# Wide tiles of a fused attention and ReGLU kernel: P1 seeded in PSUM under P2, and two quarters multiplied on VectorE straight from PSUM

## The chip, the cores and the metric

The kernel runs on one core of one Trainium2 chip. The metric is the device time of one execution in microseconds, 316.74 before the change (median of three runs, 316.7 to 316.8). Engines are named as in the profile: PE (TensorE, matmul), ACT (ScalarE), DVE (VectorE), POOL (GpSimd), SP (SyncE, which issues DMAs).

## What is computed

Sliding-window attention over 8 batches of 576 positions, 8 heads of 64, then a gated feed-forward layer on the 4608 tokens:

```python
scores = scale * np.matmul(q, k.transpose(0, 1, 3, 2))
mask = (rel >= 0) & (rel < 64)
attn = softmax(np.where(mask, scores, -1e9))
x = concat_heads(np.matmul(attn, v))          # [4608, 512]
gate = np.maximum(x @ w_gate, 0.0)            # w_gate, w_val: [512, 1536]
val = x @ w_val
out = gate * val @ w_out                      # w_out: [1536, 512]
```

## The kernel before

**Tiles.** The tokens are cut into ten tiles: tiles 0 to 3 have 384 tokens and are called narrow here, tiles 4 to 9 have 512 and are the wide ones. For a narrow tile `hidden` forms gate and value directly. For a wide tile `fast_hidden` (L555) uses a Winograd form of Strassen's scheme: seven products instead of eight, called P1 to P7, each on a half of the 512 features, a half of the tokens (256) and a half of the hidden units. Sums of weights (`us`, `vs`, made by `w_form`) and of activations (`xc`, made by `x_form`) are prepared ahead. Then `fast_output` (L667) multiplies by `w_out`, 128 tokens at a time, 12 matmuls of 512 columns each. Between these four output blocks lie the attention steps of later tiles: `values` (two per wide tile) and `scores` (two per wide tile).

**Products and quarters.** The hidden units go in three pieces, j = 0, 1, 2. For each j every product is run for the gate (i = 0) and for the value (i = 1); each time it is four matmuls of 256 columns into one PSUM bank. These four matmuls are called a group here, so a wide tile has 3 x 7 x 2 = 42 groups. P1, P6, P7 and P4 add up in one bank, "A" (L572), P2 is alone in "B", P5 and P3 add up in "C". The four quarters of a piece (half of the units, n, by half of the tokens, h) come from them so:

- n=0, h=0 is P1 + P2. ACT copies A after P1 into an SBUF tile `pr` (`snap`, L593 to L601); DVE adds bank B to it (`add`, L603, the sum at L609); ACT applies relu to the gate's sum (L615); POOL multiplies gate by value into `g_sb` (L620).
- n=0, h=1: A after P6 is copied likewise, and C after P3 is added; relu and multiplication as above.
- n=1, h=1: A after P7, plus C after P5; likewise.
- n=1, h=0 is A after P4: ACT reads both banks into SBUF, the gate with relu (`direct`, L630), and POOL multiplies (L637).

So a piece has on ACT six copies, three relus of sums and two L630; on DVE six sums; on POOL four multiplications.

P6 may overwrite A only when the copy of P1 is done, P7 when the copy of P6 is, P4 when the copy of P7 is; P3 may go on top of P5 only when DVE has read C for the P7 sum (L573).

**What sets the order.** A small planner, `Weaver`, runs while the program is written. It keeps a clock and a heap of events with due times; `W.at(t, fn)` adds one, and before each group `W.advance` issues all events that have come due, in the order of their times. Each group advances the clock by 4 x 263 / 2400 = 0.4383 us, each output matmul by 519 / 2400 = 0.216 us, `values` by 0.62 and `scores` by 0.72. So a wide tile is 42 x 0.4383 + 2 x 0.62 + 2 x 0.72 + 48 x 0.216 = 31.47 us long to the planner. The order in which instructions are issued to one engine is the order in which they run on it: ACT, DVE and POOL are queues.

The q and k transposes on DVE (L195, four for a batch) are such events too. `ahead(t)` (L874) puts them at the start of wide tile t plus `WIDE_T` = 32.69 us plus the slots 0.2, 3.4, 7.6 and 13.8, so for tiles 4 and 5 they fall into the hidden parts of tiles 5 and 6. Those that fall into tile 4 are planned at the start of tile 3, plus 27.6 and the same slots. To the planner tile 3 is 24 x 4 x 391 / 2400 + 36 x 0.216 = 23.43 us long (scores and values that are issued out of the heap do not advance the clock). Tiles 7 to 9 have no q and k transposes.

**Order of the products.** For j = 0: P1, P2, P6, P5, P7, then P1 of j = 1, P4, P3. For j = 1 and 2: P6, P2, P7, P5, P4, then P1 of the next j (if any), P3.

**PSUM banks.** There are eight banks of 128 x 512 fp32. `bank()` (L371) hands out the free bank that was freed longest ago; `free.append` gives one back at the moment when its last reader is issued. A matmul with `start=True` opens a new sum in a bank, and those without it add. `fast_hidden` opens A with P1, B with P2 and C with P5.

The names in the profile: `pr` is the SBUF tile of a pair (gate, value), `bank` a PSUM bank, `g_sb` the gated product in f16, `pw` the exponentials of the scores, `o_sb` an output block on its way to HBM. L588 is the matmul of all products, L679 the output matmul of wide tiles, L396 the exponential of the wide tiles' scores.

Of the kernel before, what the change touches and what calls it, by code (L numbers as in the profile page):

```python
# [47 lines left out]
def kernel(  # L48
# [10 lines left out]
    nc = tc.nc  # L59
# [187 lines left out]
    def st_tiles(u):  # L247
        d = units.setdefault(u, {})
        if u == 0:
            d["st"] = [one_bank() for _ in range(G)]  # L250
        else:
            halves = [two_banks() for _ in range(2)]
            d["st"] = halves[0] + halves[1]
        d["p"] = [None] * G

    def st_block(to, g, hh, n, biased=False):
# [46 lines left out]
    def u_pv(u, hhs=(0, 1), banks=None):  # L303

        d = units[u]
        if "pv" not in d:
            if banks:
                d["pv"] = [one_bank() for _ in range(2)]
            else:
                d["pv"] = two_banks()  # L310
        for hh in hhs:
            to = d["pv"][hh]
            for w in range(UB):
                b, vw = divmod(UB * u + w, NG)
                for s in range(2):
                    for j in range(G):
                        c = VW * (2 * w + s)
                        nc.tensor.matmul(  # L318
                            to[32 * j:32 * j + 32, c:c + D + 1], p_of(u, G * hh + j, w)[:, 32 * s:32 * s + 32],
                            v16s[b % 2][:, vw, G * hh + j, 0:D + 1],  # L320
                            start=True, stop=True, skip_group_check=True)
        return 0.27 * len(hhs)
# [44 lines left out]
    quads = {}  # L367
    wides = {}
    free = []

    def bank():  # L371

        while not free:
            W.pop()
        return free.pop(0)

    def read(to, give):
        unread.discard(id(to))
# [6 lines left out]
    def q_st(qd, banks=None):  # L385

        d = quads[qd] = {"st": banks or [bank() for _ in range(G)], "p": [None] * G}
        unread.update(map(id, d["st"]))
        run_rows([[st_block(d["st"][g][:, 256 * hh + 64 * i:256 * hh + 64 * i + 64], g, hh, q_window(qd, i))
                   for hh in range(2) for i in range(QW)] for g in range(G)])  # L390
        return 0.72
# [19 lines left out]
    def t_pv(t, hh, banks, give):  # L411

        if t not in wides:
            wides[t] = {"pv": {}, "give": give, "x": a_n.tile([128, 2, WS, 2, D // 2], FP16, name="xw", bufs=1),
                        "r": a_n.tile([128, 2, WS, 1], FP32, name="rw")}
        d = wides[t]
        d["pv"][hh] = banks
        unread.update(map(id, banks))
        for qh in range(2):
            qd = 2 * (t - NS) + qh  # L420
            while quads[qd].get("masked", 0) < G:
                W.pop()
            for i in range(QW):
                b, vw = divmod(q_window(qd, i), NG)
                for s in range(2):
                    n = 2 * (QW * qh + i) + s
                    to = banks[n // BS][:, VW * (n % BS):]
                    for j in range(G):
                        nc.tensor.matmul(to[32 * j:32 * j + 32, 0:D + 1],  # L429
                                         quads[qd]["p"][j][:, QW * hh + i, 32 * s:32 * s + 32],  # L430
                                         v16s[b % 2][:, vw, G * hh + j, 0:D + 1],
                                         start=True, stop=True, skip_group_check=True)
# [82 lines left out]
    def hidden(t, spans, f0=0, f1=NF, each=1):  # L515

        if t not in gs:
            gs[t] = g_sb_p.tile([128, NF, WT], FP16, name="g_sb"), {}
        g_sb, done = gs[t]
        xt = xt_tile(t)  # L520
        n = spans[0][1] - spans[0][0]

        w = 512 // n
        each = max(each, w)

        def part(tile):
            return tile[:, 0:w * n].rearrange("p (w n) -> p w n", w=w)

        def relu(r_sb, h1):
            nc.scalar.activation(part(r_sb), part(h1), ACT.Relu)  # L530

        def gate(f, c0, r_sb, h2):
            nc.vector.tensor_tensor(g_sb[:, f:f + w, c0:c0 + n], part(r_sb), part(h2), MUL)  # L533
            done.update(dict.fromkeys(range(f, f + w), c0 + n))

        for fb in range(f0, f1, each):
            r2s = [f_sb.tile([128, 2, WT], FP32, name="pr", bufs=6) for _ in range(2)]
            r_sbs = {}
            for i, wt in enumerate((wg, wv)):
                for c0, f in ((c0, f) for c0, _ in spans for f in range(fb, fb + each, w)):  # L540
                    h = one_bank()
                    for b in range(w):
                        W.advance(W.clock)
                        w_need(wt, f + b)
                        for c in range(NC):
                            nc.tensor.matmul(h[:, b * n:b * n + n], wt[:, c, (f + b) * 128:(f + b) * 128 + 128],  # L546
                                             xt[:, c, c0:c0 + n], start=(c == 0), stop=(c == NC - 1))
                        W.clock += 4 * (n + 7) / 2400.0
                    if i == 0:
                        r_sb = r_sbs[c0, f] = r2s[len(r_sbs) // 2][:, len(r_sbs) % 2]  # L550
                        W.at(W.clock, lambda r_sb=r_sb, h=h: relu(r_sb, h))
                    else:
                        W.at(W.clock, lambda f=f, c0=c0, r_sb=r_sbs[c0, f], h=h: gate(f, c0, r_sb, h))

    def fast_hidden(t):  # L555
# [14 lines left out]
                    "P6": (sums[:, 1, :, c], xc[:, 1]), "P7": (sums[:, 2, :, c], xc[:, 2])}[name]  # L570

        TO = {"P1": "A", "P6": "A", "P7": "A", "P4": "A", "P2": "B", "P5": "C", "P3": "C"}  # L572
        AFTER = {"P6": ("P1", "snap"), "P7": ("P6", "snap"), "P4": ("P7", "snap"), "P3": ("P7", "sum")}  # L573

        def product(j, name, i):
            W.advance(W.clock)
            if name in AFTER:
                before, what = AFTER[name]
                while (j, what, before, i) not in at:
                    W.pop()  # L580
            first = name in ("P1", "P2", "P5")
            if first:
                at[j, TO[name], i] = bank()
            to = at[j, TO[name], i]
            w, x = operands(name, *kinds[i], j)
            for m in range(2):
# [2 lines left out]
                                     start=(first and m == 0 and k == 0), stop=(k == 1), skip_group_check=True)  # L589
            W.clock += 4 * (HT + 7) / 2400.0  # L590
            at[j, "ran", name, i] = True

        def snap(j, name, i):  # L593
            if i == 0:
# [5 lines left out]
                at[j, "snap", name, i] = True  # L600
            W.at(W.clock, copy)  # L601

        def add(j, name, bank_name, i, n, h, delay):  # L603

            def summed():
                while (j, "snap", name, i) not in at:
                    W.pop()
                pr, to = at[j, "pair", name], at[j, bank_name, i]
                nc.vector.tensor_tensor(pr[:, i], to, pr[:, i], ADD)  # L609
                at[j, "sum", name, i] = True  # L610
                if name != "P7":
# [3 lines left out]
                        nc.scalar.activation(pr[:, 0], pr[:, 0], ACT.Relu)  # L615
                    W.at(W.clock + 1.1, relu)
                else:
                    def mult():
                        f = 2 * j + HF * n
                        nc.gpsimd.tensor_tensor(gh[:, f:f + 2, h], pair(pr[:, 0]), pair(pr[:, 1]), MUL)  # L620
                        done[f, h] = done[f + 1, h] = True
                    W.at(W.clock + 1.2, mult)
            W.at(W.clock + delay, summed)

        def direct(j, i):
            if i == 0:
                at[j, "r"] = f_sb.tile([128, 2, WT], FP32, name="pr", bufs=6)

            def copy():
                nc.scalar.activation(at[j, "r"][:, i], at[j, "A", i], ACT.Copy if i else ACT.Relu)  # L630
                free.append(at[j, "A", i])
                if i == 1:
                    W.at(W.clock + 0.7, mult)

            def mult():
                f = 2 * j + HF
                nc.gpsimd.tensor_tensor(gh[:, f:f + 2, 0], pair(at[j, "r"][:, 0]), pair(at[j, "r"][:, 1]), MUL)  # L637
                done[f, 0] = done[f + 1, 0] = True
            W.at(W.clock, copy)

        def step(j, name):
            for i in range(2):
                product(j, name, i)
                if name in ("P1", "P6", "P7"):
                    snap(j, name, i)
                if name == "P2":
                    add(j, "P1", "B", i, 0, 0, 0.1)
                if name in ("P5", "P7") and (j, "ran", "P5", i) in at and (j, "ran", "P7", i) in at:
                    add(j, "P7", "C", i, 1, 1, 0.1 if name == "P5" else 0.8)
                if name == "P4":  # L650
                    direct(j, i)
                if name == "P3":
                    add(j, "P6", "C", i, 0, 1, 0.1)

        last = NF // 4 - 1
        step(0, "P1")
        for j in range(last + 1):
            for name in ("P2", "P6", "P5", "P7") if j == 0 else ("P6", "P2", "P7", "P5"):
                step(j, name)
            tail = [(j, "P4"), (j + 1, "P1"), (j, "P3")] if j else [(j + 1, "P1"), (j, "P4"), (j, "P3")]  # L660
            for jj, name in tail:
# [5 lines left out]
    def fast_output(t, between):  # L667

        g_sb, done = gs[t]
        for sub, before in enumerate(between):  # L670
            for fn in before:
                fn()
            op = bank()
            for i, f in enumerate(F_LAST):
                if i % 4 == 0:
                    W.advance(W.clock)
# [26 lines left out]
        W.at(W.clock, evac)  # L703

    def op_tile():
        return one_bank()

    def output(t, subs=None):
        for sub in range(widths[t] // 128) if subs is None else subs:
# [262 lines left out]
```

## Time and profile before

| | |
|---|---|
| time, median of 3 runs | 316.74 us |
| span of the profiled execution, first to last instruction | 315.2 us |
| granted TensorE clock, mean over the span | 1.000 |
| ACT busy in the stretch 220.72 to 239.32 us (hidden part of tile 7) | 16.86 of 18.60 us |
| DVE busy in the same stretch | 10.70 us |
| POOL busy in the same stretch | 12.03 us |
| DVE busy in the stretch 156.04 to 175.04 us (hidden part of tile 5) | 14.92 of 19.00 us |

The span is 1.5 us shorter than the median of the timed runs, which include what lies around the instructions. A line of the groups reads: line, engine, operation, output and inputs with their shapes, count | busy time in all, mean ns of one | idle time of the engine just ahead of them and what ended it. A line of the timeline reads: start in us, length in us, engine, line, operation, output and input, and how many instructions are merged into it. A busy PE is read off the starts of its groups, since matmuls are pipelined and the length shown for a group overlaps that of the next.

### The profile page before, as it was taken

The numbers are of one execution on the slowest core, as the hardware profiler recorded it, in microseconds if no ns is written. First come the engines' busy times: TensorE is split into PE (matmuls) and PEld (weight loads), VectorE is DVE, ScalarE is ACT, GpSimd is POOL, SyncE is SP. The second block draws the span as 40 slices with busy tenths as digits, with TensorE's granted clock in tenths as the row PEclk, the third lists the DMA queues.
The fourth block names the chain that finished last, engine by engine and source line by source line (L and its number), as shares of the span: only waits on it lengthen the run. The fifth ranks groups of instructions, "written<-read, shape, count | busy, mean of one in ns | idle before, by whom it ended". The sixth has DMA issues, their size and how long they took to land.

```text
span 315.2 us, 10195 instructions
## 1 busy us (share of the span) xinstructions
PE 303.3 (96%) x4295; PEld 210.6 (67%) x4295; DVE 225.9 (72%) x413; ACT 190.1 (60%) x382; POOL 204.9 (65%) x214
## 2 busy tenths in 40 slices
PE   4899989999999998999999999999999999999995
PEld 2575947756556555885588558854886488648854
DVE  6937983786895987989788877898468846845630
ACT  3645324533616616993889378946895689529951
POOL 8859799603982009789848983887389319833860
PEclk9999999999999999999999999999999999999999
DMA  8999999929949305932990299003910200020002
GB/s 218 174 195 205 196 174 227 119 77 168 140 66 212 84 34 102 190 76 39 231 158 8 19 237 171 9 28 86 134 34 10 95 36 2 2 102 33 3 33 100
DMA packets 56749, 33.34 MB, mean 106 GB/s; under 512 B 39552, under 2 KB 48128, under 8 KB 56704
## 3 DMA queue, kind: packets, MB, share of 16 engines
q0 software_dynamic: 46688, 18.29, 50.0%
q1 hardware_dynamic: 9872, 14.34, 14.0%
q8 instruction: 33, 0.54, 0.7%
q14 instruction: 12, 0.10, 0.1%
q10 hardware_dynamic: 144, 0.07, 0.1%
HBM read 37.75 MB, written 9.44 MB: 150 GB/s over the span
## 4 chain that ended last, share of the span: by engine, by line
PE 80%; DVE 6%; DMA 4%; ACT 4%; POOL 2%; issue 2%; SPq 0%; DVEq 0%; ACTq 0%; POOLq 0%
PE bank L588 29%; PE bank L679 20%; PE bank L546 18%; PE bank L694 7%; PE bank L260 3%; PE bank L429 2%; DMA wg<-in_moe_w_gate_dram 2%; DMA v<-v 2%; DVE pr L609 2%; DVE qT L195 2%; ACT pr L599 1%; ACT pr L615 1%; POOL v L201 1%; ACT pr L630 1%; PE bank L318 1%
## 5 line engine op out<-in xcount | busy, mean ns | idle before, releaser
L620 POOL TENSOR_TENSOR g_sb<-pr 128x512 f16<-128x512 f32 x54 | 68.6, 1276 | 43.3 <-ACT pr L615 38.6
L609 DVE TENSOR_TENSOR pr<-bank,pr 128x512 f32<-128x512 f32 x108 | 69.6, 684 | 37.8 <-PE bank L588 31.4
L679 PE MATMUL bank<-wo,g_sb 128*128 128x512 f16 x276 | 62.9, 380 | 0.0
L599 ACT COPY pr<-bank 128x512 f32<-128x512 f32 x108 | 57.7, 596 | 7.7 <-PE bank L588 6.1
L679 PEld LDWEIGHTS <-g_sb 128*128 128x128 f16 x276 | 25.5, 98 | 28.9
L533 DVE TENSOR_TENSOR g_sb<-pr,bank 128x384 f16<-128x384 f32 x48 | 26.3, 550 | 21.7 <-PE bank L546 19.4
L530 ACT ACTIVATE pr<-bank 128x384 f32<-128x384 f32 x48 | 23.5, 494 | 24.5 <-PE bank L546 19.4
L684 ACT COPY o_sb<-bank 128x512 f32<-128x512 f32 x23 | 13.5, 587 | 40.4 <-PE bank L679 37.8
L546 PE MATMUL bank<-xt,wg 128*128 128x192 f16 (+1 forms) x256 | 34.9, 286 | 1.2 <-DMA wg<-in_moe_w_gate_dram 0.9
L201 POOL DMA_DIRECT2D v<-in_v_dram x41 | 34.8, 873 | 1.8 <-DMA q<-in_q_dram 1.0
L615 ACT ACTIVATE pr<-pr 128x512 f32<-128x512 f32 x54 | 34.6, 645 | 0.9 <-DVE pr L609 0.9
L546 PE MATMUL bank<-xt,wv 128*128 128x192 f16 (+1 forms) x256 | 34.5, 286 | 0.0
L694 PE MATMUL bank<-wo,g_sb 128*128 128x512 f16 x144 | 32.8, 379 | 0.1
L588 PE MATMUL bank<-xc,vs 128*128 128x256 f16 x216 | 32.4, 272 | 0.4 <-ACT pr L599 0.4
L588 PE MATMUL bank<-xc,us 128*128 128x256 f16 x216 | 32.4, 272 | 0.3
L466 POOL TENSOR_TENSOR xc<-xt 128x512 f16<-128x512 f16 x12 | 13.9, 1162 | 27.4 <-DVE xt L454 27.2
L588 PEld LDWEIGHTS <-us 128*128 128x128 f16 x288 | 28.1, 98 | 5.1 <-issue 1.8
L588 PEld LDWEIGHTS <-vs 128*128 128x128 f16 x288 | 28.1, 98 | 4.5 <-issue 0.9
L546 PEld LDWEIGHTS <-wg 128*128 128x128 f16 x256 | 22.7, 98 | 10.3 <-DMA wg<-in_moe_w_gate_dram 1.4
L546 PEld LDWEIGHTS <-wv 128*128 128x128 f16 x256 | 22.8, 98 | 8.0
L396 ACT ACTIVATE pw<-bank 128x512 f16<-128x512 f32 x48 | 25.4, 605 | 3.3 <-PE bank L260 3.0
L401 DVE TENSOR_TENSOR pw<-pw,mask 128x512 f16<-128x512 f16 x48 | 22.6, 500 | 5.5 <-ACT pw L396 4.7
(76 smaller groups left out, 461.7 us busy)
## 6 DMA issues: line engine op xcount, KB each, us to landing
out_dram<-o_sb SPq DMA_DIRECT2D x35, 256.0 KB, 3.4
k<-in_k_dram POOLq DMA_DIRECT2D x15, 288.0 KB, 5.5
q<-in_q_dram POOLq DMA_DIRECT2D x15, 288.0 KB, 7.6
v<-in_v_dram POOLq DMA_DIRECT2D x31, 128.0 KB, 6.8
v<-v SPq DMA_DIRECT2D x14, 132.0 KB, 3.4
v<-v SPq DMA_DIRECT2D x28, 66.0 KB, 2.8
wg<-in_moe_w_gate_dram POOLq DMA_DIRECT2D x6, 256.0 KB, 6.8
wv<-in_moe_w_val_dram POOLq DMA_DIRECT2D x6, 256.0 KB, 8.1
```

The lines of the kernel that those rows point to most:

```text
L201: nc.gpsimd.dma_start(v16s[b % 2][lo:hi, g, :, 0:64], v[b, :, 64 * g - 64 + lo:64 * g - 64 + hi].rearrange("h p d -> p h d"))
L396: nc.scalar.activation(d["p"][g].rearrange("p n c -> p (n c)"), d["st"][g], ACT.Exp, scale=scale)
L530: nc.scalar.activation(part(r_sb), part(h1), ACT.Relu)
L533: nc.vector.tensor_tensor(g_sb[:, f:f + w, c0:c0 + n], part(r_sb), part(h2), MUL)
L546: nc.tensor.matmul(h[:, b * n:b * n + n], wt[:, c, (f + b) * 128:(f + b) * 128 + 128], xt[:, c, c0:c0 + n], start=(c == 0), stop=(c == NC ...
L588: nc.tensor.matmul(to[:, HT * m:HT * m + HT], w[:, k, 128 * m:128 * m + 128], x[:, k], start=(first and m == 0 and k == 0), stop=(k == 1), ...
L599: nc.scalar.copy(pr[:, i], at[j, "A", i])
L609: nc.vector.tensor_tensor(pr[:, i], to, pr[:, i], ADD)
L615: nc.scalar.activation(pr[:, 0], pr[:, 0], ACT.Relu)
L620: nc.gpsimd.tensor_tensor(gh[:, f:f + 2, h], pair(pr[:, 0]), pair(pr[:, 1]), MUL)
L679: nc.tensor.matmul(op, g_sb[:, f, 128 * sub:128 * sub + 128], wo[:, f], start=(i == 0), stop=(i == NF - 1))
L694: nc.tensor.matmul(op, g_sb[:, f, bass.ds(sub * 128, 128)], wo[:, f], start=(f == 0), stop=(f == NF - 1))
```

## The change

- P1 is copied by ACT not to SBUF but into the bank that will be B (`seed`), and P2 adds on top of it: P2 no longer opens its bank, and waits for the copy. The sum P1 + P2 then stands in PSUM.
- The quarters P1 + P2 and P4 are both finished by `direct`: ACT applies relu to the gate's bank into an SBUF tile `r`, and DVE multiplies `r` by the value's bank straight from PSUM into `g_sb`. The DVE sums of P1 + P2, the second L630 copy and two of the four POOL multiplications are gone.
- A matmul without `start` adds only where the bank has been fully written since it was last opened. So the planner now keeps a set `written` of such banks. The seed uses a free bank that is in the set; all others use, if there is one, a free bank that is not. Attention scores and values, which write their banks in parts, remove their banks from the set; products and output blocks add theirs.
- In j = 0, P5 comes second and P2 fourth: P1, P5, P6, P2, P7.

```diff
-    def bank():
-
-        while not free:
+    written = set()
+
+    def bank(whole=False):
+
+        while not any((id(to) in written) or not whole for to in free):
             W.pop()
-        return free.pop(0)
+        to = next((to for to in free if (id(to) in written) == whole), free[0])
+        free.remove(to)
+        return to
...
-        AFTER = {"P6": ("P1", "snap"), "P7": ("P6", "snap"), "P4": ("P7", "snap"), "P3": ("P7", "sum")}
+        AFTER = {"P2": ("P1", "snap"), "P6": ("P1", "snap"), "P7": ("P6", "snap"), "P4": ("P7", "snap"), "P3": ("P7", "sum")}
...
-            first = name in ("P1", "P2", "P5")
+            first = name in ("P1", "P5")
             if first:
                 at[j, TO[name], i] = bank()
+                written.add(id(at[j, TO[name], i]))
...
+        def seed(j, i):
+
+            def copy():
+                at[j, "B", i] = bank(True)
+                nc.scalar.copy(at[j, "B", i], at[j, "A", i])
+                at[j, "snap", "P1", i] = True
+            W.at(W.clock, copy)
...
+        def mult(eng, j, n, h, r, v, to=None):
+            f = 2 * j + HF * n
+            eng.tensor_tensor(gh[:, f:f + 2, h], pair(r), pair(v), MUL)
+            done[f, h] = done[f + 1, h] = True
+            if to is not None:
+                free.append(to)
...
-        def direct(j, i):
+        def direct(j, i, name, n):
+            to = at[j, name, i]
+
+            def relu():
+                r = at[j, "r", name] = f_sb.tile([128, WT], FP32, name="r", bufs=3)
+                nc.scalar.activation(r, to, ACT.Relu)
+                free.append(to)
+
             if i == 0:
-                at[j, "r"] = f_sb.tile([128, 2, WT], FP32, name="pr", bufs=6)
-
-            def copy():
-                nc.scalar.activation(at[j, "r"][:, i], at[j, "A", i], ACT.Copy if i else ACT.Relu)
-                free.append(at[j, "A", i])
-                if i == 1:
-                    W.at(W.clock + 0.7, mult)
-
-            def mult():
-                f = 2 * j + HF
-                nc.gpsimd.tensor_tensor(gh[:, f:f + 2, 0], pair(at[j, "r"][:, 0]), pair(at[j, "r"][:, 1]), MUL)
-                done[f, 0] = done[f + 1, 0] = True
-            W.at(W.clock, copy)
+                W.at(W.clock, relu)
+            else:
+                W.at(W.clock + 0.1, lambda: mult(nc.vector, j, n, 0, at[j, "r", name], to, to))
 
         def step(j, name):
             for i in range(2):
                 product(j, name, i)
-                if name in ("P1", "P6", "P7"):
+                if name == "P1":
+                    seed(j, i)
+                if name in ("P6", "P7"):
                     snap(j, name, i)
                 if name == "P2":
-                    add(j, "P1", "B", i, 0, 0, 0.1)
+                    direct(j, i, "B", 0)
                 if name in ("P5", "P7") and (j, "ran", "P5", i) in at and (j, "ran", "P7", i) in at:
-                    add(j, "P7", "C", i, 1, 1, 0.1 if name == "P5" else 0.8)
+                    add(j, "P7", i, 1, 0.1 if name == "P5" else 0.8)
                 if name == "P4":
-                    direct(j, i)
+                    direct(j, i, "A", 1)
                 if name == "P3":
-                    add(j, "P6", "C", i, 0, 1, 0.1)
+                    add(j, "P6", i, 0, 0.1)
...
-            for name in ("P2", "P6", "P5", "P7") if j == 0 else ("P6", "P2", "P7", "P5"):
+            for name in ("P5", "P6", "P2", "P7") if j == 0 else ("P6", "P2", "P7", "P5"):
                 step(j, name)
```

More of the change, by code (lines that the diff above doesn't have):

```diff
@@ L253, in st_tiles @@
             d["st"] = halves[0] + halves[1]
+        written.difference_update(map(id, d["st"]))
         d["p"] = [None] * G
@@ L310, in u_pv @@
                 d["pv"] = two_banks()
+            written.difference_update(map(id, d["pv"]))
         for hh in hhs:
@@ L388, in q_st @@
         unread.update(map(id, d["st"]))
+        written.difference_update(map(id, d["st"]))
         run_rows([[st_block(d["st"][g][:, 256 * hh + 64 * i:256 * hh + 64 * i + 64], g, hh, q_window(qd, i))
@@ L418, in t_pv @@
         unread.update(map(id, banks))
+        written.difference_update(map(id, banks))
         for qh in range(2):
@@ L541, in hidden @@
                     h = one_bank()
+                    written.discard(id(h))
                     for b in range(w):
@@ L601, in snap, with add @@
             W.at(W.clock, copy)
-        def add(j, name, bank_name, i, n, h, delay):
+        def mult(eng, j, n, h, r, v, to=None):
[4 more added lines that the diff above has]
+                free.append(to)
+        def add(j, name, i, n, delay):
             def summed():
@@ L607, in summed @@
                     W.pop()
-                pr, to = at[j, "pair", name], at[j, bank_name, i]
+                pr, to = at[j, "pair", name], at[j, "C", i]
                 nc.vector.tensor_tensor(pr[:, i], to, pr[:, i], ADD)
@@ L617, in summed @@
                 else:
-                    def mult():
[L619 to L622, printed above, removed]
-            W.at(W.clock + delay, summed)
-        def direct(j, i):
-            if i == 0:
-                at[j, "r"] = f_sb.tile([128, 2, WT], FP32, name="pr", bufs=6)
-            def copy():
-                nc.scalar.activation(at[j, "r"][:, i], at[j, "A", i], ACT.Copy if i else ACT.Relu)
-                free.append(at[j, "A", i])
-                if i == 1:
-                    W.at(W.clock + 0.7, mult)
-            def mult():
-                f = 2 * j + HF
-                nc.gpsimd.tensor_tensor(gh[:, f:f + 2, 0], pair(at[j, "r"][:, 0]), pair(at[j, "r"][:, 1]), MUL)
-                done[f, 0] = done[f + 1, 0] = True
-            W.at(W.clock, copy)
+                    W.at(W.clock + 1.2, lambda: mult(nc.gpsimd, j, n, 1, pr[:, 0], pr[:, 1]))
+            W.at(W.clock + delay, summed)
+        def direct(j, i, name, n):
[4 more added lines that the diff above has]
+                free.append(to)
+            if i == 0:
+                W.at(W.clock, relu)
+            else:
+                W.at(W.clock + 0.1, lambda: mult(nc.vector, j, n, 0, at[j, "r", name], to, to))
         def step(j, name):
@@ L673, in fast_output @@
             op = bank()
+            written.add(id(op))
             for i, f in enumerate(F_LAST):
@@ L705, in op_tile @@
     def op_tile():
-        return one_bank()
+        to = one_bank()
+        written.add(id(to))
+        return to
     def output(t, subs=None):
```

## The prediction

> **What bounds the kernel now.** I read the page first, then the busy time by stretches, then the timeline of two wide tiles.
>
> ```profile
> span 315.2 us, 10195 instructions
> ## 1 busy us (share of the span) xinstructions
> PE 303.3 (96%) x4295; PEld 210.6 (67%) x4295; DVE 225.9 (72%) x413; ACT 190.1 (60%) x382; POOL 204.9 (65%) x214
> ```
>
> PE is busy 96% of the span, so only its idle time can be won. The groups show what the change touches:
>
> ```profile
> L620 POOL TENSOR_TENSOR g_sb<-pr 128x512 f16<-128x512 f32 x54 | 68.6, 1276 | 43.3 <-ACT pr L615 38.6
> L609 DVE TENSOR_TENSOR pr<-bank,pr 128x512 f32<-128x512 f32 x108 | 69.6, 684 | 37.8 <-PE bank L588 31.4
> L679 PE MATMUL bank<-wo,g_sb 128*128 128x512 f16 x276 | 62.9, 380 | 0.0
> L599 ACT COPY pr<-bank 128x512 f32<-128x512 f32 x108 | 57.7, 596 | 7.7 <-PE bank L588 6.1
> ```
>
> The reader sees 1.28 us per POOL multiplication, 0.68 us per DVE sum, 0.60 us per ACT copy. Back to back they start closer: two sums take 1.29 us in the timeline (0.60 apart), two copies 1.07 (0.485 apart).
>
> How much is PE idle in the wide hidden parts? A product's four matmuls (a group) start 0.437 us after the group before when nothing stops PE (229.29 to 233.22 in tile 7 is nine groups). From first to last of 42 groups should be 41 x 0.437 = 17.91 us. The timeline gives 18.77 in tile 4 (123.32 to 142.09), 18.56 in tiles 5 and 6 (155.88 to 174.44, 188.22 to 206.78), 18.16 in tile 7 (220.56 to 238.72); tiles 8 and 9 have the same stretch as 7 (18.60 and 18.59 us). So PE idles 0.86, 0.65, 0.65, 0.25, 0.25, 0.25 us: **2.9 us in all, the most that this change can win.** Where it lies, in tile 7 (start, length in us):
>
> ```profile
> 231.74 1.08 ACT L630 ACTIVATE pr<-bank 128x512 f32<-128x512 f32 x2
> ...
> 233.22 0.60 PE L588 MATMUL bank<-xt,vs 128*128 128x256 f16 x4
> 233.23 1.07 ACT L599 COPY pr<-bank 128x512 f32<-128x512 f32 x2
> ...
> 233.87 0.60 PE L588 MATMUL bank<-xc,us 128*128 128x256 f16 x4
> ```
>
> P6 of j=2 may overwrite bank A only after ACT has copied P1 out. ACT is late by two L630 and one relu, and PE starts at 233.87 instead of 233.66 (and 0.04 late again on the next group). This 0.25 is in every wide tile. Tiles 5 and 6 lose 0.40 more at P3 of j=2:
>
> ```profile
> 170.81 1.29 DVE L609 TENSOR_TENSOR pr<-bank,pr 128x512 f32<-128x512 f32 x2 [0.78 <-PE bank L588]
> ...
> 172.02 1.25 DVE L195 STREAM_TRANSPOSE qT<-q 128x576 f32<-128x576 f32 x1
> ...
> 173.12 2.65 DVE L609 TENSOR_TENSOR pr<-bank,pr 128x512 f32<-128x512 f32 x4
> 173.16 0.60 PE L588 MATMUL bank<-xc,wv 128*128 128x256 f16 x4
> ...
> 173.84 0.60 PE L588 MATMUL bank<-xt,us 128*128 128x256 f16 x4
> ```
>
> P3 waits for the P7 sum (173.12 + 0.69), and that sum is queued on DVE behind a transpose, itself queued behind the two P1 sums.
>
> **The change, part by part.** Per j and wide tile, ACT goes from 11 instructions of 512 columns to 10, POOL from 4 multiplications to 2 (36 x 1.28 = 46 us less in all), DVE stays at 6 (two P1 sums become two multiplications).
>
> POOL: worth nothing by itself. No PE wait in the wide tiles is on POOL, and DVE is not faster beside an idle POOL: two sums take 1.29 at 222.14 (POOL idle) and 1.29 at 229.13 (POOL busy). No DMA and no POOL or SP issue is moved.
>
> Seeds: ACT copies P1 into bank B where it copied it to SBUF. The trace has no ACT write to PSUM. Bounds: nothing below the 0.485 spacing, and twice a copy, 1.19, above; I take 0.60, as its source and size are those of L599. P2's new wait for the seed is free, since P6 stands ahead of P2 on PE and already waits for the same instruction. With one ACT instruction less after P4, seed 0 of j=2 starts 4.34 us after P2 of j=1 and ends at 4.94; P6 is due at 5.25. **The 0.25 goes in each of six tiles.** What is late next: nothing until a seed takes 0.88.
>
> The Trainium skill, "ScalarE: Activation LUTs", § Step-by-step: what each stage is for, says that ScalarE writes PSUM faster than SBUF; no run here shows it yet. By it a seed would be under 0.60 and the sum would stay as it is.
>
> Multiplication from PSUM on DVE: L533 multiplies SBUF by PSUM into f16, 384 columns, in 0.550; L609 takes 0.684 for 512. The slope between them is 1.05 ns a column, so I take 0.68 (0.60 to the next start); bounds 0.55 and 0.69.
>
> The new wait: this multiplication needs the relu of the gate bank, an ACT instruction behind others, and what is queued behind it on DVE is the transpose and then the P7 sum that P3 needs. Before, the P1 sums needed only PE. The order follows from the planner. Its clock gains 0.4383 us per group. In tiles 5 and 6 the transposes are due 1.42, 4.62, 8.82 and 15.02 us into the tile (32.69 minus 31.47, plus the slots 0.2, 3.4, 7.6, 13.8). The multiplication of the P1+P2 quarter is due at 8 x 0.4383 + 0.1 = 3.61 (j=0) and 34 x 0.4383 + 0.1 = 15.00 (j=2), the P7 sums at 4.74 and 16.32. So at j=0 and j=2 DVE has: multiplication, transpose, P7 sum.
>
> - j=0, counted from the start of P2's first group. P2 is 4 groups later than before, P7 follows at 0.87, P3 is due at 3.50. ACT: P6 copies at -0.18 and 0.31, relu 0.79 to 1.40. DVE: multiplication 1.42, transpose 2.02, P7 sum 3.11 (1.09 after a transpose starts, as 158.07 to 159.16), done 3.80. P3 starts 0.31 late; its second group another 0.16 (the second sum starts 0.6 later, and 0.68 plus 0.03 of signal follow). **0.47; before: none.**
> - j=2, from P2 likewise. ACT: two P6 copies from -0.18, then the relu of P6's sum of j=1 (0.52 to the next), so the new relu runs 1.31 to 1.92. DVE: multiplication 1.94, transpose 2.54, P7 sum 3.63 to 4.32. P3, due at 3.50, starts 0.85 late, its second group 0.19 more. **1.04; before 0.40.**
>
> Without a transpose the P7 sum ends at 2.9 (j=0) and 3.2 (j=2), in time: tiles 7 to 9 lose nothing. The transpose at 8.82 stands ahead of its multiplication (8.87) and runs while that waits.
>
> Tile 4: its planner start is 23.43 after tile 3's, its first transpose 27.8, so 4.38 in: between multiplication (3.61) and P7 sum (4.74) of j=0, as above. Its T4 (41 groups in) is after P3. And the new bank choice: P5, now second, takes banks never fully written, here those of the last score block, whose exponentials ran at 124.00 and 124.96. P5's two groups, due 124.19 and 125.07, start at 124.63 and 125.62, and P6's second group at 126.49 where it stood at 126.11. Idle up to there 0.98, P3 0.52 (0.35 + 0.17), then none: 1.50, before 0.86. In tiles 5 to 9 these exponentials end 0.4 us or more before the tile starts (153.40 + 2.06 against 155.88).
>
> **Sum**: tile 4 +0.64; tiles 5 and 6 2 x (1.51 - 0.65) = +1.72; tiles 7 to 9 3 x -0.25 = -0.75; **+1.6 us**. The outputs after each tile have PE at full rate, and the last quarters come earlier than POOL's did, so nothing is added there. The profiled execution's span is 315.2; the median 316.74 is 1.5 more for what lies around it. 315.2 + 1.6 + 1.5 = **318.4 us**, 0.5% slower. With the multiplication at its lower bound (0.13 less, five places) it is 317.7; another 0.2 us of wait at each of the ten P3 groups and seeds would make 320.
>
> **Rivals.**
> 1. *Faster: the transposes run ahead of the multiplications.* Place: DVE at j=2 of tiles 5 and 6, where 15.00 stands against 15.02 in the planner. If the transpose is ahead there, it runs while DVE waits for the relu, and P3 waits for nothing: 0.47 - 0.65 = -0.18 per tile, in all 0.64 - 0.36 - 0.75 = -0.5, 316.3 us. If no transpose holds a P7 sum anywhere (relu and multiplication done 0.35 us sooner at j=0, 0.85 at j=2), tile 4 is +0.12, the others -0.65 or -0.25 each: -1.9, **314.8 us**. It decides when the P7 sum leaves DVE within 3.47 us of P2. For it: ACT is relieved. Against it: before, the trace has the second P1 sum (due at the same 15.00) ahead of the transpose (170.81, 172.02). Chance 0.14.
> 2. *Slow seeds.* From 0.88 us on, P6 waits at j=2, later at j=0. At 1.19, j=2 loses 0.3 + 0.7 and j=0 0.2 + 0.6, about 1.8 a tile, near 11 in all: 329 us. At 1.0 about 0.4 a tile: 321 us. Nearest rows (0.587 to 0.645) speak against. Chance 0.09.
> 3. *A draw*: P3's waits half as long, 0.8 less per tile in 5 and 6: 316.8 us. Chance 0.12.
> 4. *P2 overwrites the seed instead of adding.* The instructions and waits stay, so the time is that of the forecast, 318.4; it is counted there.
>
> **How the numbers follow.** Forecast (317.5 to 319.5) 0.65; rival 1 0.14; rival 2 0.09; draw 0.12. A measurement tells about 0.2% (0.63 us) from no change. Faster 0.14, within 0.2% 0.12, slower 0.65 + 0.09 = 0.74. The range, 316.5 to 320.0, leaves out rival 1 and most of rival 2.
>
> **What would show it.** PE waits of tiles 5 and 6 at P3, j=0 and j=2, released by the DVE P7 sum, 0.5 and 1.0 us; DVE idle in front of the new multiplication, released by the ACT relu; no wait at P6 of j=2; P5 of tile 4 released by ACT's exponential; seeds near 0.6; tiles 7 to 9 at 18.35 us. Wrong if P3 is not late, or if P6 waits for seeds.

## The result and the profile after

The changed kernel takes 318.75 us, against 316.78 for the kernel before on the same chips (medians of 20 runs each): the ratio is 1.0052 (95% interval 1.0032 to 1.0072). The forecast was 318.4. The page of the profile after, first its head, then the groups that the change touches (line numbers are those of the changed kernel: L597 is the matmul of the products, L606 the seed, L616 the copies of P6 and P7, L622 the multiplication, L633 the sums, L650 the relu out of PSUM):

```profile
span 316.7 us, 10123 instructions
## 1 busy us (share of the span) xinstructions
PE 302.8 (96%) x4295; PEld 210.5 (66%) x4295; DVE 225.6 (71%) x413; ACT 180.4 (57%) x364; POOL 160.5 (51%) x178
...
L622 POOL TENSOR_TENSOR g_sb<-pr 128x512 f16<-128x512 f32 x36 | 45.9, 1274 | 84.0 <-ACT pr L639 81.3
...
L622 DVE TENSOR_TENSOR g_sb<-r,bank 128x512 f16<-128x512 f32 x36 | 24.7, 685 | 39.4 <-ACT r L650 25.8
L633 DVE TENSOR_TENSOR pr<-bank,pr 128x512 f32<-128x512 f32 x72 | 46.1, 680 | 2.4 <-PE bank L597 2.2
L616 ACT COPY pr<-bank 128x512 f32<-128x512 f32 x72 | 38.8, 595 | 11.8 <-PE bank L597 11.7
```

The work went where it was meant to go: POOL lost 44 us and ACT 10 us, DVE kept its time. That wins nothing by itself, because PE sets the end. What is new and matters is in the idle column: DVE stands idle 25.8 us ahead of its 36 multiplications, waiting for ACT's relu. The seeds have a group of their own, in the list of groups by shape:

```profile
L606 ACT COPY bank<-bank 128x512 f32<-128x512 f32 x36 | 19.6, 581 | 0.0
```

The waits of PE (total us, times, longest) show who stops the products of the wide tiles. The kernel before has one line for them, the changed kernel two others:

```profile
PE bank L588 <- ACT pr L599: 0.4, 1, 0.4
```

```profile
PE bank L597 <- DVE pr L633: 1.8, 4, 0.7
...
PE bank L597 <- ACT pw L402: 0.7, 2, 0.4
```

This view counts a wait only from the modelled end of the matmuls ahead, so it shows less than PE loses (0.20 us at 162.80 below, where the starts give 0.36). The starts of the groups show all of it. From the first to the last start of a wide tile's 42 groups there are 17.90 us without a stop (41 x 0.4366); what is over is idle:

| idle of PE in the hidden part, us | tile 4 | tile 5 | tile 6 | tiles 7, 8, 9 | sum |
|---|---|---|---|---|---|
| before | 0.87 | 0.66 | 0.66 | 0.26 each | 3.0 |
| after | 1.50 | 1.56 | 1.56 | 0.00 each | 4.6 |

Tile 5 of the changed kernel at j=0 and then at j=2, from the timeline (start, length):

```profile
159.72 0.62 ACT L650 ACTIVATE r<-bank 128x512 f32<-128x512 f32 x1
...
160.37 0.69 DVE L622 TENSOR_TENSOR g_sb<-r,bank 128x512 f16<-128x512 f32 x1 [2.84 <-ACT r L650]
...
160.98 1.25 DVE L195 STREAM_TRANSPOSE kT<-k 128x576 f32<-128x576 f32 x1
...
162.07 1.27 DVE L633 TENSOR_TENSOR pr<-bank,pr 128x512 f32<-128x512 f32 x2
...
162.80 0.60 PE L597 MATMUL bank<-xt,us 128*128 128x256 f16 x4 [0.20 <-DVE pr L633]
```

```profile
172.13 0.60 ACT L650 ACTIVATE r<-bank 128x512 f32<-128x512 f32 x1
...
172.76 0.69 DVE L622 TENSOR_TENSOR g_sb<-r,bank 128x512 f16<-128x512 f32 x1 [1.76 <-PE bank L597]
...
173.36 1.25 DVE L195 STREAM_TRANSPOSE qT<-q 128x576 f32<-128x576 f32 x1
...
173.88 0.60 PE L597 MATMUL bank<-xc,wv 128*128 128x256 f16 x4
...
174.45 1.28 DVE L633 TENSOR_TENSOR pr<-bank,pr 128x512 f32<-128x512 f32 x2
...
175.19 0.60 PE L597 MATMUL bank<-xt,us 128*128 128x256 f16 x4 [0.71 <-DVE pr L633]
```

Each row starts when the row above lets it: the relu ends at 172.73, the multiplication starts at 172.76 (the bracket names PE, but the PE group that it needs had long been done; the relu came last), the transpose 0.60 after it, the P7 sum 1.09 after that, and P3 starts 0.05 after that sum's first half, 1.31 us after the group ahead (173.88) in place of 0.44. At j=0 P3 is 0.36 late, its second group 0.16 more.

In tile 4, P5's two groups wait for the exponentials of the scores whose banks they were given:

```profile
123.74 0.60 ACT L402 ACTIVATE pw<-bank 128x512 f16<-128x512 f32 x1
...
124.48 0.60 PE L597 MATMUL bank<-xc,us 128*128 128x256 f16 x4 [0.39 <-ACT pw L402]
```

### The profile page after: what moved, and what is told of

It is laid out like the page before. It is cut to its first block, busy times and chain, and to the rows that moved or that the text cites. A ratio compares the mean times of both kernels' runs of the same rounds, so it can differ in the third digit from the quotient of the medians.

```text
span 316.7 us, 10123 instructions
## 1 busy us (share of the span) xinstructions
PE 302.8 (96%) x4295; PEld 210.5 (66%) x4295; DVE 225.6 (71%) x413; ACT 180.4 (57%) x364; POOL 160.5 (51%) x178
## 4 chain that ended last, share of the span: by engine, by line
PE 84%; DVE 9%; ACT 3%; issue 1%; DMA 1%; POOL 0%; DVEq 0%; ACTq 0%
PE bank L597 30%; PE bank L699 19%; PE bank L554 19%; PE bank L714 7%; PE bank L261 3%; PE bank L436 2%; DVE kT L195 2%; DVE p L300 1%; PE bank L320 1%; DVE qT L195 1%; DMA vs<-in_k_dram 1%; DVE g_sb L622 1%; DVE pr L633 1%; PE bank L746 1%; ACT pr L616 1%
## 5 line engine op out<-in xcount | busy, mean ns | idle before, releaser
L622 POOL TENSOR_TENSOR g_sb<-pr 128x512 f16<-128x512 f32 x36 | 45.9, 1274 | 84.0 <-ACT pr L639 81.3
L622 DVE TENSOR_TENSOR g_sb<-r,bank 128x512 f16<-128x512 f32 x36 | 24.7, 685 | 39.4 <-ACT r L650 25.8
L633 DVE TENSOR_TENSOR pr<-bank,pr 128x512 f32<-128x512 f32 x72 | 46.1, 680 | 2.4 <-PE bank L597 2.2
L616 ACT COPY pr<-bank 128x512 f32<-128x512 f32 x72 | 38.8, 595 | 11.8 <-PE bank L597 11.7
L597 PE MATMUL bank<-xc,us 128*128 128x256 f16 x216 | 32.4, 273 | 0.4 <-ACT pw L402 0.4
L597 PE MATMUL bank<-xc,vs 128*128 128x256 f16 x216 | 32.4, 273 | 0.3 <-ACT pw L402 0.3
L597 PEld LDWEIGHTS <-us 128*128 128x128 f16 x288 | 28.1, 98 | 6.7 <-issue 3.5
L597 PEld LDWEIGHTS <-vs 128*128 128x128 f16 x288 | 28.1, 98 | 4.6 <-issue 1.3
L639 ACT ACTIVATE pr<-pr 128x512 f32<-128x512 f32 x36 | 22.9, 636 | 7.7 <-DVE pr L633 7.7
```

The source lines that it names most:

```text
L597: nc.tensor.matmul(to[:, HT * m:HT * m + HT], w[:, k, 128 * m:128 * m + 128], x[:, k], start=(first and m == 0 and k == 0), stop=(k == 1), ...
L616: nc.scalar.copy(pr[:, i], at[j, "A", i])
L622: eng.tensor_tensor(gh[:, f:f + 2, h], pair(r), pair(v), MUL)
```

## The experiments

**Theory.** PE loses time where the P7 sum leaves DVE late, because it is queued behind a transpose, and this behind a multiplication that waits for ACT's relu; and in tile 4 through the choice of banks. The wait at P6 of j=2 went because ACT has one instruction less after P4. **Rivals**: the loss lies in PSUM (bank pressure, or reads by DVE and ACT beside each other); the transposes cost their DVE time wherever they stand; the seeds, not the P4 part, relieve P6.

Each experiment gives the time, its ratio to the kernel before, run again beside it, with the 95% interval, and PE's idle time in tiles 4 / 5 / 6 / each of 7 to 9, read as above.

**1. The last transpose ahead of the multiplication**

```diff
-        SLOTS = (0.2, 3.4, 7.6, 13.8)
+        SLOTS = (0.2, 3.4, 7.6, 13.6)
```

> The changed kernel with only the last q/k transpose of a batch planned 0.2 us earlier (slot 13.6 for 13.8), so that on DVE it stands ahead of the multiplication of P1+P2 at j=2 in tiles 5 and 6, not behind it. Theory (queue order: multiplication waits for the relu, transpose behind it, P7 sum behind both): the P3 wait at j=2 goes, 1.03 us in each of two tiles, the waits at j=0 (0.52) stay; span 316.7 - 2.1 = 314.6, time 318.75 - 2.1 = 316.7. Rival (the lost time comes from PSUM: bank pressure, or DVE's reads of PSUM beside ACT's): the order of a transpose changes nothing, 318.7.

Measured: 316.57 us, 0.9988 (0.9969 to 1.0007); idle 1.49 / 0.52 / 0.52 / 0. The wait at j=2 is gone whole, that at j=0 stays as it was. A change of 0.2 us in one planned time is worth the 2.1 us that the theory gives it. For these 2.1 us the PSUM rival falls: the edit changes no bank and no access to PSUM.

**2. The same transpose behind the P7 sums**

```diff
-        SLOTS = (0.2, 3.4, 7.6, 13.8)
+        SLOTS = (0.2, 3.4, 7.6, 15.6)
```

> The changed kernel with the same transpose planned 1.8 us later (slot 15.6), behind both P7 sums at j=2 of tiles 5 and 6. Theory: again no P3 wait at j=2, span 314.6, time 316.7, though the transpose now runs later; the multiplication of P4 and the P6 sums come 1.1 us later, which the attention values and the first output blocks cover. Rival (a transpose costs PE its DVE time wherever it stands near the end of the tile): P3 or the output is late by about as much as before, 318.7.

Measured: 316.68 us, 0.9994 (0.9981 to 1.0007); idle 1.49 / 0.52 / 0.52 / 0. Tile 5 of this kernel:

```profile
174.61 1.28 DVE L633 TENSOR_TENSOR pr<-bank,pr 128x512 f32<-128x512 f32 x2
...
175.55 0.60 PE L597 MATMUL bank<-xt,us 128*128 128x256 f16 x4
175.81 1.25 DVE L195 STREAM_TRANSPOSE qT<-q 128x576 f32<-128x576 f32 x1
175.99 0.60 PE L597 MATMUL bank<-xt,vs 128*128 128x256 f16 x4
176.89 0.68 DVE L622 TENSOR_TENSOR g_sb<-r,bank 128x512 f16<-128x512 f32 x1
```

P3 (175.55) waits for nothing, and the multiplication of P4 that now stands behind the transpose costs nothing: from the last group of tile 5 to the first of tile 6 it is 13.81 us, as in the changed kernel. (From tile 4 to tile 5 it is 14.25 here, 13.88 there; the extra lies in a stop between score matmuls at 154.7 for which the profile shows no cause.) It is not the transpose's 1.25 us that PE pays for, only its place between a late instruction and the sum.

**3. Two transposes ahead**

```diff
-        SLOTS = (0.2, 3.4, 7.6, 13.8)
+        SLOTS = (0.2, 2.2, 7.6, 13.6)
```

> The changed kernel with two transposes planned earlier (slots 2.2 for 3.4 and 13.6 for 13.8), ahead of the multiplications of P1+P2 at j=0 and j=2. Theory: tiles 5 and 6 lose nothing any more at P3, 2 x 1.55 = 3.1 us less: span 313.6, time 315.65, which is 1.1 less than before the change. In tile 4, whose transposes have other due times, nothing changes (1.5 us idle). Rival (PSUM): 318.7.

Measured: 315.47 us, 0.9956 (0.9942 to 0.9970); idle 1.51 / 0 / 0 / 0. Tiles 5 and 6 lose nothing. DVE idles where it idled before, with the transpose out of the way:

```profile
170.49 1.25 DVE L195 STREAM_TRANSPOSE qT<-q 128x576 f32<-128x576 f32 x1
171.71 0.60 ACT L650 ACTIVATE r<-bank 128x512 f32<-128x512 f32 x1
172.34 0.69 DVE L622 TENSOR_TENSOR g_sb<-r,bank 128x512 f16<-128x512 f32 x1 [0.59 <-PE bank L597]
172.94 1.28 DVE L633 TENSOR_TENSOR pr<-bank,pr 128x512 f32<-128x512 f32 x2
```

The transpose runs while the multiplication would wait for the relu anyway, and the sum follows 0.60 after the multiplication.

**4. The same slots in the kernel before**

The edit of experiment 3, in the kernel before.

> The kernel before with these two slots (2.2 and 13.6) and nothing else. Theory: no gain, since there the first P1 sum is ready 0.6 us earlier and two P1 sums and a transpose stand ahead of the P7 sum in either order; P6 keeps its 0.25 wait in each tile and P3 of j=2 its 0.40 in tiles 5 and 6; 316.8 (316.4 to 317.2). Rival (the slots were simply badly placed for either kernel): 0.8 less, 316.0.

Measured: 317.26 us, 1.0010 (0.9988 to 1.0032); idle 0.87 / 0.66 / 0.66 / 0.26, as before. So these two slots win nothing in the kernel before: there the last transpose now stands between the two P1 sums and no longer behind both, and the P7 sum comes no sooner. A slot still earlier (13.2) takes P3's 0.40 away in experiment 10, with the P4 part in; in the kernel before by itself it was not run, so part of what experiments 9 and 10 win may be had without the change.

**5. The P4 quarter alone** (in the kernel before: relu on ACT for i = 0, multiplication from PSUM on DVE for i = 1, `to` is bank A; P1 + P2 as before)

```diff
-                nc.scalar.activation(at[j, "r"][:, i], at[j, "A", i], ACT.Copy if i else ACT.Relu)
+                nc.scalar.activation(at[j, "r"], to, ACT.Relu)
...
-                nc.gpsimd.tensor_tensor(gh[:, f:f + 2, 0], pair(at[j, "r"][:, 0]), pair(at[j, "r"][:, 1]), MUL)
+                nc.vector.tensor_tensor(gh[:, f:f + 2, 0], pair(at[j, "r"]), pair(to), MUL)
```

> One part of the change alone: the kernel before, with the P4 quarter read from PSUM (relu on ACT, multiplication on DVE) in place of two ACT reads and a POOL multiplication. P1+P2 stays as before. Theory: one ACT instruction less after P4, so the 0.25 wait at P6 of j=2 goes in six tiles; the P7 sum is not behind a multiplication, so P3 loses only its old 0.40 in tiles 5 and 6; 316.97 - 1.5 = 315.4. Rival (multiplying from PSUM on DVE is itself what slows the tile): 317 or more.

Measured: 315.78 us, 0.9954 (0.9931 to 0.9976); idle 0.61 / 0.40 / 0.40 / 0. P6's wait at j=2 is gone from all six tiles; P3's old 0.40 stays in two, and P6's wait at the start of tile 4 (0.61) stays. This part alone makes the kernel faster.

**6. The seed alone** (in the changed kernel: `direct_sbuf` has P4 read by ACT twice and multiplied on POOL, as before)

```diff
-                    direct(j, i, "A", 1)
+                    direct_sbuf(j, i)
```

> The other part alone: the changed kernel with P4 handled as before the change (two ACT reads, POOL multiplies). Theory: all P3 and P5 waits of the changed kernel stay (4.6 us in all), and the 0.25 wait at P6 of j=2 is back in six tiles, as ACT again has 11 instructions per j: 318.75 + 1.5 = 320.2. Rival (the seed in PSUM is what relieves P6, the P4 part what delays P3): 315 to 317.

Measured: 320.21 us, 1.0102 (1.0068 to 1.0137); idle 1.69 / 1.77 / 1.77 / 0.26, 0.50, 0.26. P6's 0.26 is back (tile 8 loses 0.23 more at P3 of j=2, which no other run shows), the P3 and P5 waits stay. So the two parts about add up, in idle time: the P4 part wins 1.5 us, and the seed, with the multiplication behind it and the order and the banks that come with it, loses 3.3; together 1.8, where the whole change lost 1.7.

**7. Each seed copied twice**

```diff
-                nc.scalar.copy(at[j, "B", i], at[j, "A", i])
+                for _ in range(2):
+                    nc.scalar.copy(at[j, "B", i], at[j, "A", i])
```

> The changed kernel with each seed copied twice, the same data to the same bank; the output is unchanged. Theory (a seed has 0.3 us of room at P6 of j=2 and 0.4 at j=0, a second copy takes 0.49): P6 waits for the seeds at j=2 by about 0.7 and at j=0 by about 0.6 us, 1.3 a tile, and the relu of P1+P2 and with it P3 in tiles 4 to 6 come later too: 8 us more, 327 (324 to 330). Rival (ACT has room after 18.6 us of work were taken from it): 319.

Measured: 331.08 us, 1.0439 (1.0395 to 1.0483); idle 3.40 / 3.33 / 3.32 / 2.31, 2.31, 2.30. The waits of PE:

```profile
PE bank L597 <- ACT bank L607: 5.4, 11, 0.5
```

PE waits for the seeds, as the theory said, but the size was missed by 4 us and the time lies outside the range that was given. One reason is the price of a copy: the four copies at 229.12 (two banks, each copied twice) take 2.29 us, since the second copy of a bank starts 0.61 to 0.64 after the first, when that has ended, and not 0.49. In tiles 7 to 9 P6 loses 0.87 at j=0 and 0.87 at j=2 (0.22 at its first group, 0.65 at its second), not 0.6 and 0.7; and 0.55 more is lost at j=1 at P6, P7 and P4, which I had not counted. ACT is busy 18.45 of 20.21 us of tile 7 there, so little is left to catch up in. The sum of idle time over the changed kernel's, 17.0 - 4.6 = 12.4 us, is the 12.3 us of the times.

**8. The relu ahead on ACT**

```diff
-                        W.at(W.clock + 1.1, relu)
+                        W.at(W.clock + (1.6 if name == "P6" else 1.1), relu)
```

> The changed kernel with the relu of the P6 sum planned 0.5 us later, so that on ACT the relu of P1+P2 at j=2 stands ahead of it, not behind. Theory (DVE's multiplication waits for this relu, and the transpose and the P7 sum wait behind the multiplication): at j=2 of tiles 5 and 6 the multiplication starts 0.5 us sooner and P3 waits 0.5 instead of 1.03 us; j=0 is unchanged; 318.75 - 1.05 = 317.7. Rival (the multiplication waits for P2 or for DVE, not for ACT): 318.75.

In this kernel the last piece's quarter n=0, h=1 is multiplied (in tile 5 at 176.94) before its gate's sum has had its relu (178.24); the instructions are the same in number. Measured: 317.58 us, 1.0018 (0.9998 to 1.0039); idle 1.49 / 0.93 / 0.93 / 0. At j=2 of tile 5:

```profile
171.45 0.62 ACT L650 ACTIVATE r<-bank 128x512 f32<-128x512 f32 x1
...
171.94 0.64 ACT L639 ACTIVATE pr<-pr 128x512 f32<-128x512 f32 x1
...
172.10 0.69 DVE L622 TENSOR_TENSOR g_sb<-r,bank 128x512 f16<-128x512 f32 x1 [1.19 <-ACT r L650]
...
173.80 1.27 DVE L633 TENSOR_TENSOR pr<-bank,pr 128x512 f32<-128x512 f32 x2
...
174.53 0.60 PE L597 MATMUL bank<-xt,us 128*128 128x256 f16 x4
```

With the two relus changed about, the multiplication starts 0.03 after its relu's end again, and P3's wait falls from 1.03 to 0.46. So the relu on ACT is what the DVE queue waits for, and what it comes sooner goes through to PE.

**9. All mended**

```diff
-        SLOTS = (0.2, 3.4, 7.6, 13.8)
+        SLOTS = (0.2, 2.2, 7.6, 13.6)
...
-                qk_ahead(NS + 2, T + 27.6, SLOTS, 6.0)
+                qk_ahead(NS + 2, T + 26.6, SLOTS, 6.0)
...
-        to = next((to for to in free if (id(to) in written) == whole), free[0])
+        to = free[0] if oldest else next((to for to in free if (id(to) in written) == whole), free[0])
...
-                at[j, TO[name], i] = bank()
+                at[j, TO[name], i] = bank(oldest=name == "P5")
```

> The changed kernel with three things mended: slots 2.2 and 13.6, the transposes of tile 4 planned 1.0 us earlier (26.6 for 27.6 after tile 3's start), so that the first stands ahead of the multiplication at j=0, and P5 taking the bank freed longest ago, so that in tile 4 it does not wait for an exponential. Theory: PE idle in the wide hidden parts is only P6's wait for ACT at the start of tile 4, 0.6 us of the 4.6 of the changed kernel; 318.75 - 4.0 = 314.7, below the kernel before by 2.2. Rival (PSUM has no room for the seeds in tile 4, and another bank is late): no better than with the two slots alone, 315.5.

Measured: 314.57 us, 0.9934 (0.9922 to 0.9946), the lowest median of all; idle 0.65 / 0 / 0 / 0. In tile 4 both P3's waits and all but 0.06 of P5's are gone, so the transpose and the bank each were what the theory said. What is left is P6's wait in tile 4, now for a seed:

```profile
PE bank L597 <- ACT bank L606: 0.4, 1, 0.4
```

**10. Without seeds, one transpose ahead** (experiment 5 with another slot)

```diff
-        SLOTS = (0.2, 3.4, 7.6, 13.8)
+        SLOTS = (0.2, 3.4, 7.6, 13.2)
```

> The kernel before with the P4 quarter read from PSUM and the last transpose planned 0.6 us earlier (slot 13.2), ahead of both P1 sums at j=2; no seeds. Theory: P3's 0.40 in tiles 5 and 6 goes as well, and PE idle is again 0.6 us, in tile 4; 315.78 - 0.8 = 315.0, so the seeds win nothing that this kernel does not have. Rival (the seeds relieve DVE or ACT enough to matter): 0.5 or more above the kernel with all three things mended.

Measured: 314.90 us, 0.9956 (0.9941 to 0.9972); idle 0.61 / 0 / 0 / 0. The intervals of 9 and 10 overlap, and PE's idle time is the same: these runs show nothing that seeding P1 in PSUM wins beyond the P4 part and one slot. (The medians differ by 0.3 us, which the intervals do not tell from nothing.)

## Why the prediction was right

- *Nothing but PE's idle time counts.* Right. Over the twelve kernels the idle time ran from 0.6 to 17.0 us and the times from 314.6 to 331.1 with it: each time less its idle time is between 313.8 and 314.4. That leaves no room to speak of for the 44 us less on POOL.
- *The 0.25 at P6 goes.* Right: tiles 7 to 9 run 17.90 us from first to last start, where it was 18.16. It comes from the P4 part alone (experiments 5 and 6).
- *P3 at j=0.* 0.47 forecast, 0.52 measured. *P3 at j=2.* 1.04 forecast, 1.03 measured. The links were each seen: the relu (8), the place of the transposes (1, 2, 3).
- *Tile 4.* 1.50 forecast and measured. P5's two waits were 0.56 and 0.48, where 0.44 and 0.55 had been worked out; the first exponential ended at 124.34, and P5 started 0.14 later rather than 0.03. P3 lost 0.47, forecast 0.52. The causes are those forecast; that the total agrees to 0.01 is luck, as the misses cancel.
- *Seeds take 0.60.* 0.581. The Trainium skill, "ScalarE: Activation LUTs", § Step-by-step: what each stage is for, says that ScalarE writes PSUM faster than SBUF; the trace agrees, by little: 0.581 against 0.595 for the copies from the same kind of bank into SBUF. That is the mean length of one; two seeds in a row take 1.07 to 1.09 us, as two copies do.
- *Multiplication 0.68.* 0.685.
- *Nothing is added between the hidden parts.* Nearly: from the last group of tile 4 to the first of tile 5 it is 13.88 us where it was 13.79; the others differ by 0.03 or less.
- *The sum.* +1.6 forecast, 4.6 - 3.0 = +1.6 in idle time, +1.5 in the spans, +1.97 in the medians (1.0 to 2.3 by the interval). From the first start of tile 4 to the last of tile 9 it is 179.45 us where it was 177.66, so +1.8: the idle time and 0.12 between the hidden parts. The span shows less because the wide tiles started 0.27 sooner in that execution. Whether the 0.2 us from there to the medians are more than scatter is open.
- *Rival 1* was not what happened, but its prices hold: with the one transpose turned about (316.3 forecast) 316.57 was measured. With no transpose in the way anywhere, 314.8 was forecast; experiment 9 gave 314.57, but it also took P5's waits away, which that price had left in (0.98 in tile 4, where 0.65 was measured), so like for like it is about 314.9. *Rival 2*: 329 us for seeds of 1.19; with two copies, which end 1.19 after the first has started, it was 331. The price had left out the waits at j=1. *Rival 3*, a draw, fell: P3's waits came whole.

## What to carry to other kernels

Work taken from an engine is worth only what the engine that sets the end had waited for it: 44 us on POOL won nothing, one ACT instruction less after P4 won 0.25 us at each P6. What an edit does to the order of the queues can cost. Where a change makes an instruction wait for one more engine, look at what stands behind it in its own queue and who waits for that: here a 1.25 us transpose, planned 0.02 us behind the multiplication, turned a late relu into 1 us of PE, where 0.4 had been lost. Once a change is in, plan its neighbours again: the same edit with a few transposes moved and P5's bank chosen otherwise is 0.7% faster than the kernel before, not 0.5% slower.

## What the runs showed of the hardware

A multiplication on DVE with one input in PSUM takes 685 ns for 128x512, as a sum does (680), whether POOL works beside it or not (686 in the 14 that had a POOL multiplication beside them for more than half of their length, 685 in the other 22). ACT copies PSUM to PSUM in 581 ns, and a matmul can add on top of what it wrote: P1 + P2 came out of such banks in the changed kernel. A relu moved ahead of another on ACT, 0.5 us in the plan, let DVE and with it PE go on as much sooner (P3's wait fell from 1.03 to 0.46).
